# Finer pieces at the two ends of a fused attention and SwiGLU kernel, side work moved and divided, and a list schedule built in 24 passes

## The chip, the cores and the metric

The kernel runs on one core of one Trainium2 chip. The metric is the device time of one execution in microseconds (us). A kernel's time is the median of its runs. The engines are TensorE (matmuls; PE in the profile, its weight loads PEld), VectorE (DVE), ScalarE (ACT), GpSimd (POOL) and SyncE (SP), which issues the transfers.

## The reference, cut to what matters

```python
# x: [1, 2048, 1024] bf16, all weights bf16
xn = layernorm(x)
qkv = xn @ wqkv                                  # 32 heads of 32
phi = lambda t: where(t > 0, t + 1, exp(t)) + 1e-6
kv, z = einsum(phi(k), v), sum(phi(k))           # linear attention: one state per head
s = ((phi(q) @ kv) / (phi(q) @ z + 1e-6)) @ wo
g = silu((silu(xn @ w_gate) * (xn @ w_up)) @ w_down)      # 1024 -> 3584 -> 1024
return x + s * g
```

## The kernel before

The kernel does its large products with seven-product block algorithms (two levels in places), so VectorE and ScalarE have much to do beside TensorE: sums and differences of operand blocks ("combinations"), moves and corrections of the partial results in PSUM. The program is first written down as a list of operations with what each reads and writes. A small list scheduler inside the kernel then builds one fixed instruction stream per engine from its own estimates of times. At run time each engine follows its stream in order.

The rule by which the scheduler picks, for every engine but TensorE:

```python
def schedule(self):
    ...                                  # cut: deadlines o.dl, from TensorE's work and the successors
    while len(order) < total:
        for e in self.ENGS:
            t = free[e]
            ...                          # cut: TensorE, in program order within a window of 6
            rdy = [o for o in a if o.ready <= t]
            o = (min(rdy, key=lambda o: (o.dl - o.boost, o.idx)) if rdy
                 else min(a, key=lambda o: (o.ready, o.dl)))
            ...                          # cut: take the engine that can start first
```

`boost` is zero throughout. The first x tile, its transposes, and the combinations:

```python
def x_load(i):                           # one 256 KB transfer on SyncE's queue
    dma([], [s.r], s.ap(), xf[i * 128:(i + 1) * 128, :], dsem("x%d" % s.k), 256 * KB).urgent = 10.0

# in ln_tile: two statistics over 512 columns, then one normalise over 1024
# in t_tile: tile 0 in two groups of 4 transposes, tiles 1 to 3 in one group of 8;
#            every PSUM copy of the first group goes to ScalarE

def combos(v):                           # four operations over 128 x 2048
    tt(..., v["T3"][0], v["R11"][0], v["R01"][0], ALU.subtract, True)
    tt(..., v["T1"][0], v["R01"][0], v["R00"][0], ALU.subtract, True)
    tt(..., v["T2"][0], v["R11"][0], v["T1"][0], ALU.subtract, True)
    tt(..., v["T4"][0], v["R10"][0], v["T2"][0], ALU.subtract, True)
```

Each `tt` is one elementwise operation on VectorE. Side work is hung on named steps of the block products. `recip` makes the reciprocal of the attention's denominator, `normalise_part` scales q with it (4 ScalarE scalings and 4 VectorE products each time), `combos(QV)` and `x_inner` prepare q for the product with the folded `kv @ wo`:

```python
if (k, n) == ("u", 1):
    at = {"2_1": [partial(recip, p)]}
if n == 2:
    at = {w: [partial(normalise_part, p, "gu".index(k), h)] for h, w in enumerate(("2_1", "7_1"))}
if (k, n) == ("g", 3):
    at = {"2_1": [partial(combos, QV)], "7_1": [partial(x_inner, QV, qin, QIN_AT)]}
```

The program ends by testing every transfer's semaphore on SyncE:

```python
for s in semn.values():
    if id(s) in PL.count:
        prog["sp"].append(("w", s, PL.count[id(s)]))
```

Of the kernel before, what the change touches and what calls it, by code (L numbers as in the profile page):

```python
# [10 lines left out]
ALU = mybir.AluOpType  # L11
# [7 lines left out]
TABLE, DMA_SLACK = 1.28, 2.0  # L19
# [14 lines left out]
class Plan:  # L34
# [71 lines left out]
    def schedule(self):  # L106
# [9 lines left out]
        for o in ops:  # L116
            if o.sem is not None and o.succs:
                k = bisect_right(cum, o.dl - self.lead) - 1
                if k >= 0 and pes[k] not in o.preds:
                    o.preds.add(pes[k])  # L120
                    pes[k].succs.append(o)
        for o in ops:
# [13 lines left out]
        while len(order) < total:  # L136
            best = None
            for e in self.ENGS:
# [17 lines left out]
                else:  # L156
                    rdy = [o for o in a if o.ready <= t]
                    o = min(rdy, key=lambda o: (o.dl - o.boost, o.idx)) if rdy else min(a, key=lambda o: (o.ready, o.dl))
# [29 lines left out]
        return order  # L188
# [55 lines left out]
def build_kernel(nc, A_x, A_wqkv, A_wo, B_w_gate, B_w_up, B_w_down, out, WINDOW=6, NWARM=14, NPE=4, LEAD=12.0):  # L244
# [12 lines left out]
    with ExitStack() as es:  # L257
# [220 lines left out]
        def combos(v):  # L478
            tt([v["R11"][1], v["R01"][1]], [v["T3"][1]], v["T3"][0], v["R11"][0], v["R01"][0], ALU.subtract, True)
            tt([v["R01"][1], v["R00"][1]], [v["T1"][1]], v["T1"][0], v["R01"][0], v["R00"][0], ALU.subtract, True)  # L480
            tt([v["R11"][1], v["T1"][1]], [v["T2"][1]], v["T2"][0], v["R11"][0], v["T1"][0], ALU.subtract, True)
            tt([v["R10"][1], v["T2"][1]], [v["T4"][1]], v["T4"][0], v["R10"][0], v["T2"][0], ALU.subtract, True)
# [179 lines left out]
        def x_load(i):  # L662
            s = x_ring.take()
            xslot[i] = s
            dma([], [s.r], s.ap(), xf[i * 128:(i + 1) * 128, :], dsem("x%d" % s.k), 256 * KB).urgent = 10.0
# [9 lines left out]
        def ln_tile(i):  # L675
# [4 lines left out]
            o0 = dve([s.r], [sA], lambda h: h.bn_stats(stats[:, j, 0, :], xa[:, 0:512]), 512)  # L680
            if i == 1:
                o0.preds.add(first_var[0])
                first_var[0].succs.append(o0)
            dve([s.r], [sB], lambda h: h.bn_stats(stats[:, j, 1, :], xa[:, 512:1024]), 512)
# [8 lines left out]
            if i < 2:  # L693
                dve([s.r, mvr, rsr], [o.r], lambda h: h.tensor_scalar(
                    oa, xa, mv[:, j, 0:1], rstd[:, j, :], ALU.subtract, ALU.mult), 1024, 2.6)
# [10 lines left out]
        def t_tile(i):  # L706
# [10 lines left out]
            for q, halves in enumerate(((0, 4), (4, 4)) if i == 0 else ((0, 8),)):  # L717
                k0, n = halves
                b = tb[(i + q) % 2]
                pb = ps[b][:, 0:n * 64].bitcast(FP16).rearrange("p (k t) -> p k t", t=128)  # L720
                pe_tr([s.r, ident_r], [bank_r[b]],
                      [(pb[:, k, :], xa[:, (k0 + k) * 128:(k0 + k + 1) * 128], ident[:, :]) for k in range(n)])
                xr = xt_r(i, k0, n)
                if q == 0 or i == 0:
# [42 lines left out]
        for q in range(4):  # L767
            pool([], [named("vx1", q), vx_r[q], pool_chain], lambda h, q=q: h.memset(vext[q][:, :, 128:129], 1.0))
# [14 lines left out]
        def p_piece(i, w, j):  # L783
            b = balloc(True)
            for k in range(2):
                ap, r = KVV[w]["R%d%d" % (k, j)]
                pe_mm([xt_r(i, 4 * k, 4), r], [bank_r[b]],
                      [(ps[b][:, :], xt_ap(i, 4 * k + q), ap[:, q, :], k + q == 0, k + q == 4) for q in range(4)])
# [55 lines left out]
        for n, (fn, args) in enumerate(((x_load, (0,)), (x_load, (1,)), (wkv_load, (0, 1, 0)), (wkv_load, (0, 1, 1)),  # L844
# [419 lines left out]
        class Down:  # L1264
# [107 lines left out]
            def do(self, t):  # L1372
# [15 lines left out]
                elif t[-1] == "q":  # L1388
# [3 lines left out]
                    tick()  # L1392
                elif t[0] == "4":
# [3 lines left out]
                else:  # L1397
                    w = int(t[2])
                    self.sets[w].step(int(t[0]))
                    if t[0] == "6":  # L1400
                        self.s3(w)
                    tick()
                for fn in self.at.get(t, ()):
                    fn()

# [7 lines left out]
            def fin(self, w, i, j, g):  # L1413
                p, c = self.p, 2 * self.h + w
                last = (p, c) == (1, 3)
# [29 lines left out]
                def turn():  # L1445
                    if not tbank:
                        tbank.append(balloc_part())
                    b = tbank[0]
                    pb = ps[b][:, 0:256].bitcast(FP16).rearrange("p (m n) -> p m n", n=128)
                    pe_tr([g.r, ident_r], [bank_r[b]], [(pb[:, m, :], g.ap(FP16)[:, m * 128:(m + 1) * 128], ident[:, :])  # L1450
                                                           for m in range(4)])
# [3 lines left out]
                if last and (i, j) == (1, 0):  # L1455
                    defer(2, turn)
# [41 lines left out]

        tbank = []
# [41 lines left out]
        for p in range(2):  # L1541
            for k, n in order:
# [10 lines left out]
                if (k, n) == ("u", 1):  # L1553
                    at = {"2_1": [partial(recip, p)]}
# [85 lines left out]
```

## Time and profile before

| | before |
|---|---|
| time, median of the runs | 726.71 us |
| span of the profiled execution | 725.4 us |
| TensorE busy | 707.0 us, 97% |
| VectorE, ScalarE busy | 633.8 and 402.7 us |
| first useful matmul | 8.1 us |
| TensorE's gaps over 0.3 us between 15 and 705 us | 10, together 8.3 us |
| last matmul to the end | 5.8 us |

The page of the kernel before begins as follows. The first line below has busy time, share of the span and number of instructions of each engine. The lines of digits give the busy share in tenths for 40 slices of the span. The last line is the chain of work that ended last, by engine.

```profile
span 725.4 us, 11190 instructions
PE 707.0 (97%) x4096; PEld 387.4 (53%) x4110; DVE 633.8 (87%) x1501; ACT 402.7 (56%) x773; POOL 14.2 (2%) x35
...
PE   7999999999999999999999999999999999999996
...
DVE  6999968989999998988966999999999989797852
...
PE 87%; DVE 8%; DMA 2%; ACT 1%; issue 1%; SPq 0%; DVEq 0%
```

TensorE is the limit and the only thing to win is its gaps. The page can't size them well: the Trainium skill ("Perfetto Trace Analysis", Per-engine timelines, Tensor Engine Instruction) says that a matmul's end in the profile is estimated and not observed. The start is observed, so the gaps here are distances between matmul starts, less one beat: 216 ns for 512 columns, 109 ns for 256, the medians of this trace. Gaps of exactly one more beat at 512 columns, one every 10 us, are missing records and stay out by the limit of 0.3 us: this trace has 14 of them and 4096 matmul records for 4110 weight loads, 14 too few.

The waits of TensorE between 15 and 705 us in the kernel before (who waited for whom, us in total, times, longest):

```profile
PE ps L233 <- DVE ps L376: 3.6, 6, 1.0
PE ps L233 <- ACT ps L365: 1.8, 2, 0.9
PE ps L233 <- ACT TM L365: 1.0, 1, 1.0
PE ps L233 <- DVE W L376: 0.3, 1, 0.3
```

All are waits for VectorE or ScalarE, not for transfers. Where those engines stand full is shown by the stretches of the kernel before (busy us of each engine in 20 us, then the granted clock, the DMA share and GB/s):

```profile
220.00:240.00 20.00, 18.54 (x102) 9.44 (x100) 19.93 (x47) 19.26 (x40) 0.00 (x0) 1.00 0.48 135
400.00:420.00 20.00, 19.05 (x97) 9.24 (x96) 19.97 (x46) 4.51 (x10) 0.00 (x0) 1.00 0.95 250
```

The columns after the first are PE, PEld, DVE, ACT, POOL. At 220 to 240 us both VectorE and ScalarE are full while q is scaled. The timeline there, kernel before (start, duration, engine, line, what; in brackets the idle time before it and its releaser):

```profile
232.29 1.35 ACT L365 ACTIVATE H<-H,zc 128x512 bf16<-128x512 bf16 x2
...
233.24 1.03 PE L233 MATMUL ps<-X,W 128*128 128x512 f16 x4
233.52 1.10 ACT L365 ACTIVATE TM<-ps 128x512 f16<-128x512 f32 x2
...
234.40 1.22 DVE L376 TENSOR_TENSOR H<-H 128x2048 f16<-128x2048 f16 x1
234.47 0.64 ACT L365 ACTIVATE ps<-ps 128x512 f32<-128x512 f32 x1
...
235.16 1.90 PE L233 MATMUL ps<-X,W 128*128 128x512 f16 x8 [0.90 <-ACT ps L365]
...
235.74 1.22 DVE L376 TENSOR_TENSOR H<-H 128x2048 f16<-128x2048 f16 x1
...
236.87 0.69 DVE L376 TENSOR_TENSOR ps<-ps,TM 128x512 f32<-128x512 f32 x1
...
237.62 1.04 PE L233 MATMUL ps<-X,W 128*128 128x512 f16 x4 [0.56 <-DVE ps L376]
```

Read it as a queue. ScalarE finishes scalings of q (`H<-H,zc`) and two evictions before it comes to the PSUM copy at 234.47 that TensorE waits for, and TensorE loses 0.90 us. Then VectorE runs a combination of 1.22 us at 235.74, and the addition that TensorE waits for starts only when it is over: another 0.56 us. The combination is only half of that wait: the addition's last input, from ScalarE, was there at 236.60 us, so without the combination it would have started some 0.3 us earlier. The Trainium skill ("TensorE: Matmul & The Clock Gate", the table at its head and "Engine queue depths") says that ScalarE's and VectorE's queues are strictly first in, first out; these lines agree, for nothing overtakes the 1.22 us operation.

At the start, kernel before:

```profile
7.36 0.55 POOL L689 TENSOR_TENSOR rstd<-veps,neg_half 128x1 f32<-128x1 f32 x1 [0.97 <-DVE veps L686]
...
8.25 1.23 DVE L376 TENSOR_TENSOR H<-H 128x2048 f16<-128x2048 bf16 x1 [0.97 <-DMA H<-in_A_wqkv_dram]
9.39 0.54 DVE L694 TENSOR_SCALAR W<-W,mv,rstd 128x1024 f16<-128x1024 bf16 x1
...
12.14 0.61 PE L240 MATMUL ps<-ident,W 128*128 128x128 f16 x8
12.34 0.60 ACT L365 ACTIVATE TM<-ps 128x512 f16<-128x512 f32 x1 [1.69 <-PE ps L233]
...
12.83 1.02 ACT L365 ACTIVATE X<-ps 128x1024 f16<-128x1024 f16 x1
...
13.91 5.35 PE L233 MATMUL ps<-H,X 128*128 128x512 bf16 x23 [1.16 <-ACT X L365]
```

TensorE waits 1.16 us for ScalarE's copy of the whole second tile. And at the end, kernel before:

```profile
718.31 0.60 ACT L365 ACTIVATE TM<-ps 128x512 f16<-128x512 f32 x1 [2.42 <-PE ps L233]
718.93 0.43 DVE L376 TENSOR_TENSOR TM<-TM 128x512 f16<-128x512 f16 x1 [2.26 <-ACT TM L365]
...
719.42 0.40 PE L240 MATMUL ps<-ident,TM 128*128 128x128 f16 x4 [1.15 <-DVE TM L376]
719.85 0.42 DVE L376 TENSOR_TENSOR TM<-ps,TM 128x512 bf16<-128x512 f16 x1 [0.49 <-PE ps L240]
```

Behind the last addition (it ends at 720.27) SyncE issues two stores of 256 KB and then runs 47 semaphore waits one after another, from 721.28 to 724.96 us. The views above leave such instructions out; their records in the trace stand about 60 ns apart even where nothing is waited for.

### The profile page before, as it was taken

To read this page: it belongs to the slowest core of one execution; us is meant where nothing else is said; L and a number is where in the kernel's file an instruction comes from. 1 tells how busy PE (TensorE), PEld (TensorE's weight loads), DVE (VectorE), ACT (ScalarE), POOL (GpSimd) and SP (SyncE) were. 2 spreads that over 40 slices of the span, in tenths; PEclk is the share of its full clock that TensorE was granted. 3 is DMA by queue.
4 is the path that set the end of the run, shared out by engine and by line. 5 is a ranking of instruction groups with operands and counts; after the bars stand their busy time and mean duration, and the time that the engine had idled before them with its cause. 6 is when DMAs were issued, how large, how long until landed. Compare 5 with 4: busy or idle time off the path is not lost.

```text
span 725.4 us, 11190 instructions
## 1 busy us (share of the span) xinstructions
PE 707.0 (97%) x4096; PEld 387.4 (53%) x4110; DVE 633.8 (87%) x1501; ACT 402.7 (56%) x773; POOL 14.2 (2%) x35
## 2 busy tenths in 40 slices
PE   7999999999999999999999999999999999999996
PEld 3544445555555555556555454555555555565642
DVE  6999968989999998988966999999999989797852
ACT  3777554887659666654212156766786656531211
POOL 3101000000000000000000000000000000000000
PEclk9999999999999999999999999999999999999998
DMA  9345235145456343326595954231915241747563
GB/s 306 100 88 106 41 116 174 59 135 200 147 159 166 100 139 123 105 67 177 141 187 161 270 149 140 59 117 61 234 59 175 87 145 61 196 114 180 129 150 94
DMA packets 139127, 98.25 MB, mean 135 GB/s; under 512 B 33344, under 2 KB 136000, under 8 KB 139072
## 3 DMA queue, kind: packets, MB, share of 16 engines
q1 hardware_dynamic: 139072, 97.54, 47.9%
q8 instruction: 32, 0.52, 0.3%
q14 instruction: 23, 0.19, 0.1%
HBM read 77.59 MB, written 12.71 MB: 124 GB/s over the span
## 4 chain that ended last, share of the span: by engine, by line
PE 87%; DVE 8%; DMA 2%; ACT 1%; issue 1%; SPq 0%; DVEq 0%
PE ps L233 87%; DVE W L376 2%; DVE H L376 2%; DVE X L376 1%; DMA P<-x_scratch 1%; DMA H<-in_A_wqkv_dram 1%; DVE ps L376 1%; DVE TM L376 1%; SPq L379 0%; DVE P L376 0%; ACT TM L365 0%; ACT H L365 0%; PE ps L240 0%; ACT L365 0%; ACT ps L365 0%
## 5 line engine op out<-in xcount | busy, mean ns | idle before, releaser
L233 PE MATMUL ps<-X,W 128*128 128x512 f16 (+1 forms) x1344 | 289.9, 354 | 3.2 <-DVE ps L376 2.3
L365 ACT ACTIVATE TM<-ps 128x512 f16<-128x512 f32 (+2 forms) x353 | 186.1, 549 | 105.2 <-PE ps L233 103.1
L233 PE MATMUL ps<-H,W 128*128 128x512 f16 (+2 forms) x1090 | 218.4, 351 | 0.7 <-DVE ps L376 0.4
L376 DVE TENSOR_TENSOR W<-W 128x1024 f16<-128x1024 bf16 (+5 forms) x416 | 184.9, 479 | 5.5 <-PE ps L233 4.9
L233 PEld LDWEIGHTS ps<-X,W 128*128 128x128 f16 (+1 forms) x1344 | 130.4, 98 | 108.6 <-DVE ps L376 4.6
L233 PEld LDWEIGHTS ps<-H,W 128*128 128x128 f16 (+1 forms) x1096 | 106.6, 98 | 95.6 <-DVE ps L376 1.4
L365 ACT ACTIVATE ps<-ps 128x512 f32<-128x512 f32 (+1 forms) x172 | 84.7, 492 | 104.8 <-PE ps L233 101.3
L376 DVE TENSOR_TENSOR ps<-ps,TM 128x256 f32<-128x256 f32 (+1 forms) x250 | 130.7, 525 | 13.8 <-PE ps L233 12.5
L233 PE MATMUL ps<-P,W 128*128 128x256 f16 (+1 forms) x516 | 99.8, 319 | 1.2 <-ACT ps L365 0.9
L365 ACT ACTIVATE H<-ps 128x512 f16<-128x512 f32 (+1 forms) x126 | 75.0, 604 | 45.6 <-PE ps L233 45.5
L376 DVE TENSOR_TENSOR H<-H 128x1024 f16<-128x1024 f16 (+6 forms) x110 | 68.9, 640 | 1.1 <-DMA H<-in_A_wqkv_dram 1.0
L365 ACT ACTIVATE TM<-TM 128x512 f16<-128x512 f32 (+1 forms) x61 | 38.0, 629 | 52.6 <-DVE TM L376 52.6
L233 PEld LDWEIGHTS ps<-P,W 128*128 128x128 f16 (+1 forms) x516 | 50.0, 98 | 31.3 <-ACT ps L365 1.6
L233 PE MATMUL ps<-W 128*128 128x256 f16 (+1 forms) x330 | 62.1, 282 | 1.1 <-DVE ps L376 1.0
L376 DVE TENSOR_TENSOR H<-H,TM 128x512 f16<-128x512 f16 x112 | 45.1, 416 | 15.1 <-ACT H L365 14.9
L376 DVE TENSOR_TENSOR TM<-ps,TM 128x512 f32<-128x512 f32 (+1 forms) x60 | 40.7, 678 | 15.6 <-PE ps L233 15.1
L233 PEld LDWEIGHTS ps<-W 128*128 128x128 f16 (+1 forms) x330 | 31.5, 98 | 33.8 <-DVE ps L376 1.9
L233 PE MATMUL ps<-H,X 128*128 128x512 bf16 (+1 forms) x147 | 35.2, 379 | 2.2 <-ACT X L365 1.6
L233 PE MATMUL ps<-H,P 128*128 128x512 bf16 (+1 forms) x108 | 26.4, 379 | 0.1
L376 DVE TENSOR_TENSOR H<-ps,TM 128x512 f16<-128x512 f32 (+1 forms) x35 | 23.8, 680 | 2.2 <-PE ps L233 2.0
L233 PEld LDWEIGHTS ps<-H,X 128*128 128x128 f16 (+1 forms) x150 | 14.2, 98 | 18.5 <-ACT X L365 2.0
L376 DVE TENSOR_TENSOR TM<-TM,W 128x512 f16<-128x512 f16 (+1 forms) x39 | 14.1, 362 | 11.5 <-ACT TM L365 11.4
(95 smaller groups left out, 426.6 us busy)
## 6 DMA issues: line engine op xcount, KB each, us to landing
W<-in_B_w_gate_dram SPq DMA_DIRECT2D x14, 1024.0 KB, 5.3
W<-in_B_w_up_dram SPq DMA_DIRECT2D x13, 1024.0 KB, 5.6
W<-in_B_w_down_dram SPq DMA_DIRECT2D x14, 896.0 KB, 6.3
W<-in_A_x_dram SPq DMA_DIRECT2D x16, 256.0 KB, 3.0
H<-in_A_wqkv_dram SPq DMA_DIRECT2D x8, 512.0 KB, 8.0
H<-r_scratch SPq DMA_DIRECT2D x32, 128.0 KB, 3.8
W<-m_scratch SPq DMA_DIRECT2D x4, 1024.0 KB, 6.0
s_scratch<-TM SPq DMA_DIRECT2D x32, 128.0 KB, 2.6
```

Source lines behind the costliest of these rows:

```text
L233: last = h.matmul(o, l, r, start=st, stop=sp, skip_group_check=True)
L365: q = PL.op("act", reads, writes, lambda h: h.activation(o, i, func, **kw), nel(o) / (1000.0 if "bias" in kw or not isinstance(kw.get("sca ...
L376: return dve(reads, writes, lambda h: h.tensor_tensor(o, a, b, op), nel(o), 1.92 if fast else 0.96)
```

## The change

The intent is to close TensorE's gaps: begin sooner, end in smaller pieces, and give VectorE and ScalarE an order that keeps TensorE fed. It has five parts: start, end, places (where side work is hung), halves (the divided combinations) and search.

Search: the schedule is built 24 times; after each pass, operations that held TensorE up get a `boost` ("lift"), and the pass with the earliest modelled end is kept. An engine may also stay idle for a much more urgent operation that is ready before the chosen one would end ("hold").

```diff
+        best = None
+        for n in range(PASSES):                       # 24
+            end = self.place()
+            if best is None or end < best[0] - 0.01:
+                best = (end, self.order, {o: (o.start, o.done) for o in ops})
+            if n + 1 < PASSES:
+                self.lift()
 ... cut: lift(), which walks back up to 12 steps from every modelled TensorE gap over 0.15 us
-                    o = min(rdy, key=lambda o: (o.dl - o.boost, o.idx)) if rdy else min(a, ...)
+                    while rdy:
+                        o = min(rdy, key=lambda o: (o.dl - o.boost, o.idx))
+                        q = [q for q in soon if q.ready + HOLD < t + o.busy and q.dl - q.boost + YIELD < o.dl - o.boost] if e != "sp" else ()
+                        if not q:
+                            break
+                        rdy.remove(o)
```

Start:

```diff
+            for h, e in enumerate(("sp", "act")):     # x tile 0: two halves on two queues
+                u = s.sub(h * KB, KB)
 ... cut
+            n = (2, 4, 8, 8)[i]                       # transposes per group, by tile
+            for q, k0 in enumerate(range(0, KT, n)):
 ... cut: normalise in two halves; copies shared between ScalarE and VectorE; tile 1's two
 ... statistics both behind tile 0's; first weight block ahead of x tile 1; first product by quarters
```

Halves, and places:

```diff
-            tt(..., v["T3"][0], v["R11"][0], v["R01"][0], ALU.subtract, True)     # and three more
+            for o, a, b in (("T3", "R11", "R01"), ("T1", "R01", "R00"), ("T2", "R11", "T1"), ("T4", "R10", "T2")):
+                for h in range(2):
 ... cut
-                    at = {"2_1": [partial(recip, p)]}
-                if n == 2:
-                    at = {w: [partial(normalise_part, p, "gu".index(k), h)] for h, w in enumerate(("2_1", "7_1"))}
+                    at = {"j1d": [partial(recip, p)]}
+                if (k, n) == ("g", 2):
+                    at = {"j1a": [partial(normalise_part, p, 0, 0)], "2_1": [partial(normalise_part, p, 0, 1)]}
+                if (k, n) == ("u", 2):
+                    at = {"j1a": [partial(normalise_part, p, 1, 0)], "2_1": [partial(normalise_part, p, 1, 1)], "4_1": [partial(combos, QV)]}
                 if (k, n) == ("g", 3):
-                    at = {"2_1": [partial(combos, QV)], "7_1": [partial(x_inner, QV, qin, QIN_AT)]}
+                    at = {"2_1": [partial(x_inner, QV, qin, QIN_AT)]}
```

End: the last down block is done in two halves of 256 columns, each with its own activation, product, transposes and a 128 KB store with a new semaphore (`oz0`, `oz1`).

```diff
+                for h, b in enumerate((self.sets[1].b, self.b2)):
+                    for n in range(0, NPAIR, 2):
+                        pe_mm([wr, tr], [bank_r[b]], [(ps[b][:, 0:256], wv[:, n + k, :],
+                                                       tv[:, k, 256 * h:256 * h + 256], False, n + k == NPAIR - 1)
+                                                      for k in range(2)])
+                        if turns and n == 2:
+                            self.turn0()
+                        if turns and n == 8:
+                            turn(turns.pop())
 ... cut: activation, product, and the turn (transposes, addition, store) of the half
```

More of the change, by code (lines that the diff above doesn't have):

```diff
@@ L16 @@
 GRAN = 256
-TABLE, DMA_SLACK = 1.28, 2.0
+PASSES, LIFT = 24, 2.0
+TABLE, DMA_SLACK, HOLD, YIELD = 1.28, 2.0, 0.1, 10
 class Op:
@@ L121, in schedule, with lift, place @@
                     pes[k].succs.append(o)
+        best = None
[5 more added lines that the diff above has]
+                self.lift()
+        self.order = best[1]
+        for o, (a, b) in best[2].items():
+            o.start, o.done = a, b
+        return self.order
+    def lift(self):
+        prev, last = {}, {}
+        for o in self.order:
+            prev[o] = last.get(o.eng)
+            last[o.eng] = o
+        for o in self.order:
+            p = prev[o]
+            if o.eng != "pe" or p is None or o.start - p.start - p.busy < 0.15:
+                continue
+            c = o
+            for _ in range(12):
+                late = max(c.preds, key=lambda p: p.done, default=None)
+                if late is None:
+                    break
+                if c.eng not in ("pe", "sp") and c.start - max(c.ready, late.done) > 0.02:
+                    c.boost += LIFT
+                c = late
+    def place(self):
+        ops = self.ops
         for o in ops:
@@ L157, in schedule @@
                     rdy = [o for o in a if o.ready <= t]
-                    o = min(rdy, key=lambda o: (o.dl - o.boost, o.idx)) if rdy else min(a, key=lambda o: (o.ready, o.dl))
+                    soon = [o for o in a if o.ready > t]
+                    while rdy:
+                        o = min(rdy, key=lambda o: (o.dl - o.boost, o.idx))
+                        q = [q for q in soon if q.ready + HOLD < t + o.busy and q.dl - q.boost + YIELD < o.dl - o.boost] if e != "sp" else ()
+                        if not q:
+                            break
+                        rdy.remove(o)
+                    if not rdy:
+                        o = min(soon or a, key=lambda o: (o.ready, o.dl))
                 s = max(t, o.ready)
@@ L187, in schedule @@
         self.order = order
-        return order
+        return max(o.done for o in ops)
     def emit(self, esem):
@@ L478, in combos @@
         def combos(v):
-            tt([v["R11"][1], v["R01"][1]], [v["T3"][1]], v["T3"][0], v["R11"][0], v["R01"][0], ALU.subtract, True)
-            tt([v["R01"][1], v["R00"][1]], [v["T1"][1]], v["T1"][0], v["R01"][0], v["R00"][0], ALU.subtract, True)
-            tt([v["R11"][1], v["T1"][1]], [v["T2"][1]], v["T2"][0], v["R11"][0], v["T1"][0], ALU.subtract, True)
-            tt([v["R10"][1], v["T2"][1]], [v["T4"][1]], v["T4"][0], v["R10"][0], v["T2"][0], ALU.subtract, True)
+            for o, a, b in (("T3", "R11", "R01"), ("T1", "R01", "R00"), ("T2", "R11", "T1"), ("T4", "R10", "T2")):
+                for h in range(2):
+                    w = {}
+                    for nm in (o, a, b):
+                        ap, r = v[nm]
+                        n = len(r.keys) // 2
+                        w[nm] = ap[:, 2 * h:2 * h + 2, :], Region(r.keys[n * h:n * h + n])
+                    tt([w[a][1], w[b][1]], [w[o][1]], w[o][0], w[a][0], w[b][0], ALU.subtract, True)
         wz = TM.at(0, 1 * KB, FP16)
@@ L664, in x_load @@
             xslot[i] = s
-            dma([], [s.r], s.ap(), xf[i * 128:(i + 1) * 128, :], dsem("x%d" % s.k), 256 * KB).urgent = 10.0
+            if i:
+                dma([], [s.r], s.ap(), xf[i * 128:(i + 1) * 128, :], dsem("x%d" % s.k), 256 * KB).urgent = 10.0
+                return
+            for h, e in enumerate(("sp", "act")):
+                u = s.sub(h * KB, KB)
+                o, q = u.ap(), xf[0:128, h * 512:h * 512 + 512]
+                PL.op(e, [], [u.r], lambda h, o=o, q=q: h.dma_start(o, q), 0.47, sem=dsem("x%d" % (4 * h)),
+                      nbytes=128 * KB)
         def wkv_load(w, j, k):
@@ L679, in ln_tile @@
             sA, sB, mvr, ver, rsr, nmr = (named(n, j) for n in ("sA", "sB", "mv", "ve", "rs", "nm"))
-            o0 = dve([s.r], [sA], lambda h: h.bn_stats(stats[:, j, 0, :], xa[:, 0:512]), 512)
+            oA = dve([s.sub(0, KB).r], [sA], lambda h: h.bn_stats(stats[:, j, 0, :], xa[:, 0:512]), 512)
+            oB = dve([s.sub(KB, KB).r], [sB], lambda h: h.bn_stats(stats[:, j, 1, :], xa[:, 512:1024]), 512)
             if i == 1:
-                o0.preds.add(first_var[0])
-                first_var[0].succs.append(o0)
-            dve([s.r], [sB], lambda h: h.bn_stats(stats[:, j, 1, :], xa[:, 512:1024]), 512)
+                for o in (oA, oB):
+                    o.preds.add(first_var[0])
+                    first_var[0].succs.append(o)
             dve([sA, sB], [mvr], lambda h: h.bn_aggr(mv[:, j, :], stats[:, j, :, :]), 60)
@@ L693, in ln_tile @@
             if i < 2:
-                dve([s.r, mvr, rsr], [o.r], lambda h: h.tensor_scalar(
-                    oa, xa, mv[:, j, 0:1], rstd[:, j, :], ALU.subtract, ALU.mult), 1024, 2.6)
+                n = 512
+                for c in range(0, 1024, n):
+                    dve([s.r, mvr, rsr], [o.sub(2 * c, 2 * n).r], lambda h, c=c: h.tensor_scalar(
+                        oa[:, c:c + n], xa[:, c:c + n], mv[:, j, 0:1], rstd[:, j, :], ALU.subtract, ALU.mult), n, 2.6)
             else:
@@ L716, in t_tile @@
                 tb.extend((balloc_part(), balloc_part()))
-            for q, halves in enumerate(((0, 4), (4, 4)) if i == 0 else ((0, 8),)):
-                k0, n = halves
-                b = tb[(i + q) % 2]
+            n = (2, 4, 8, 8)[i]
+            for q, k0 in enumerate(range(0, KT, n)):
+                b = (tb + kvb)[q] if i == 0 else tb[(i + q) % 2]
                 pb = ps[b][:, 0:n * 64].bitcast(FP16).rearrange("p (k t) -> p k t", t=128)
-                pe_tr([s.r, ident_r], [bank_r[b]],
+                pe_tr([s.sub(k0 * 256, n * 256).r, ident_r], [bank_r[b]],
                       [(pb[:, k, :], xa[:, (k0 + k) * 128:(k0 + k + 1) * 128], ident[:, :]) for k in range(n)])
                 xr = xt_r(i, k0, n)
-                if q == 0 or i == 0:
+                if q % 2 == 0 or i == 0:
                     act([bank_r[b]], [xr], dst[:, k0:k0 + n], pb, ACT.Identity)
@@ L767, in build_kernel @@
         for q in range(4):
-            pool([], [named("vx1", q), vx_r[q], pool_chain], lambda h, q=q: h.memset(vext[q][:, :, 128:129], 1.0))
+            pool([], [named("vx1", q), vx_r[q], pool_chain], lambda h, q=q: h.memset(vext[q][:, :, 128:129], 1.0), 0.13)
         def k_evac(i, j, ap, r, kind):
@@ L784, in p_piece @@
             b = balloc(True)
-            for k in range(2):
-                ap, r = KVV[w]["R%d%d" % (k, j)]
-                pe_mm([xt_r(i, 4 * k, 4), r], [bank_r[b]],
-                      [(ps[b][:, :], xt_ap(i, 4 * k + q), ap[:, q, :], k + q == 0, k + q == 4) for q in range(4)])
+            n = 2 if (i, w, j) == (0, 0, 1) else 4
+            for k0 in range(0, KT, n):
+                ap, r = KVV[w]["R%d%d" % (k0 // 4, j)]
+                pe_mm([xt_r(i, k0, n), r], [bank_r[b]],
+                      [(ps[b][:, :], xt_ap(i, k), ap[:, k % 4, :], k == 0, k == KT - 1) for k in range(k0, k0 + n)])
             if w == 0:
@@ L842, in kv_set @@
             return st
-        for n, (fn, args) in enumerate(((x_load, (0,)), (x_load, (1,)), (wkv_load, (0, 1, 0)), (wkv_load, (0, 1, 1)),
+        for n, (fn, args) in enumerate(((x_load, (0,)), (wkv_load, (0, 1, 0)), (x_load, (1,)), (wkv_load, (0, 1, 1)),
                                         (wkv_load, (0, 0, 0)), (wkv_load, (0, 0, 1)), (x_load, (2,)),
@@ L1392, in do @@
                     tick()
+                elif t == "4_1" and (self.p, self.h) == (1, 1):
+                    self.finish()
                 elif t[0] == "4":
@@ L1401, in do @@
                         self.s3(w)
+                    if t == "7_1" and (self.p, self.h) == (1, 1):
+                        b = self.sets[1].b
+                        self.b2 = balloc()
+                        act([bank_r[b]], [bank_r[self.b2], bank_r[b]], ps[self.b2][:, 0:256], ps[b][:, 256:512], ACT.Identity)
                     tick()
@@ L1404, in do, with finish, turn @@
                     fn()
+            def finish(self):
+                p, c, (i, j) = 1, 3, (1, 0)
+                wv, wr = self.S[1][4]
+                sf = sf_rings[self.link].take()
+                dma([named("s", p, c, i)], [sf.r], sf.ap(FP16), s_scr[p, c, i, :, j * 512:j * 512 + 512],
+                    dsem("sf%s%d" % (sf.a.name, sf.off // KB)), 128 * KB)
+                g = fin_rings[self.link].take()
+                q, seen = self.xo[1, j]
+                xv = q.ap().rearrange("p (m n) -> p m n", n=256)
+                turns = []
+                def turn(h):
+                    gh = g.sub(h * KB // 2, KB // 2)
+                    b = balloc_part()
+                    pb = ps[b][:, 0:128].bitcast(FP16).rearrange("p (m n) -> p m n", n=128)
+                    pe_tr([gh.r, ident_r], [bank_r[b]], [(pb[:, m, :], gh.ap(FP16)[:, m * 128:(m + 1) * 128],
+                                                          ident[:, :]) for m in range(2)])
+                    v = xv[:, 2 * h:2 * h + 2, :]
+                    vr = q.sub(h * KB, KB).r
+                    tt([bank_r[b], vr], [vr], v[:, :, 128:256], pb, v[:, :, 128:256], ALU.add)
+                    row = p * 1024 + h * 256
+                    dma([vr], [], of[row:row + 256, c * 256:(c + 1) * 256].rearrange("(m p) n -> p m n", p=128), v,
+                        dsem("oz%d" % h), 128 * KB)
+                for h, b in enumerate((self.sets[1].b, self.b2)):
+                    for n in range(0, NPAIR, 2):
+                        tv, tr = self.t4[n // 2]
+                        pe_mm([wr, tr], [bank_r[b]], [(ps[b][:, 0:256], wv[:, n + k, :],
[5 more added lines that the diff above has]
+                            turn(turns.pop())
+                    gh, sh = g.sub(h * KB // 2, KB // 2), sf.sub(h * KB // 2, KB // 2)
+                    act([bank_r[b]], [gh.r], gh.ap(FP16), ps[b][:, 0:256], ACT.Silu)
+                    tt([gh.r, sh.r], [gh.r], gh.ap(FP16), gh.ap(FP16), sh.ap(FP16), ALU.mult, True)
+                    turns.append(h)
+                turn(1)
             def keep(self, w):
@@ L1414, in fin @@
                 p, c = self.p, 2 * self.h + w
-                last = (p, c) == (1, 3)
                 sf = sf_rings[self.link].take()
@@ L1445, in turn @@
                 def turn():
-                    if not tbank:
-                        tbank.append(balloc_part())
-                    b = tbank[0]
+                    b = balloc_part()
                     pb = ps[b][:, 0:256].bitcast(FP16).rearrange("p (m n) -> p m n", n=128)
                     pe_tr([g.r, ident_r], [bank_r[b]], [(pb[:, m, :], g.ap(FP16)[:, m * 128:(m + 1) * 128], ident[:, :])
-                                                           for m in range(4)])
+                                                        for m in range(4)])
                     tt([bank_r[b], q.r], [q.r], xv[:, :, i * 128:i * 128 + 128], pb[:, :, :],
@@ L1454, in turn @@
                     done()
-                if last and (i, j) == (1, 0):
-                    defer(2, turn)
+                if (p, self.h, w, i, j) == (1, 1, 0, 1, 0):
+                    self.turn0 = turn
                 else:
@@ L1497, in down @@
             last_pair[0] = nxt
-        tbank = []
         combos(XV[0])
```

## The prediction

> **What bounds the kernel now.** The profile page has TensorE busy 707.0 of 725.4 us (97%), VectorE 87%, ScalarE 56%; the chain of waits is 87% TensorE. Only gaps in TensorE's stream can be won. By the starts of its 4,096 matmul records (216 ns apart at 512 columns, 109 at 256) they come to about 15 us; lone gaps of one beat, every 10 us, look like missing records and are left out.
>
> - Start, 5 us. Eight warm-up matmuls stand 427 ns apart, then 216: the cold clock of the Trainium skill ("TensorE: Matmul & The Clock Gate", Part 1), and the trace agrees. Then waits for the first normalised tile (transposes at 7.4 us, first useful matmul at 8.1), a weight DMA (0.5, at 11.3), ScalarE's copy of the second transposed tile (1.3, at 13.9).
> - Middle, 8.5 us: at 135 us (1.1; ScalarE's table load), 234-237 and 533-536 (1.8 each; scaling of q, ScalarE and VectorE over 19 busy of 20 us), 415 (1.1; VectorE's order), 438-443 (1.9; table load, VectorE), 655 (0.5).
> - End: 1.3 us before the last transposes. From the last matmul (719.6) to the end, 5.8 us: an addition, two 256 KB stores, and a run of about 48 SyncE waits, 60 ns each, that starts only after the last issue.
>
> **What the change does.**
> 1. Start: x tile 0 comes in halves on two queues, its normalise, transposes and copies go in pieces, and tile 1's statistics no longer delay tile 0's (0.65 us of VectorE): first useful matmul near 6.7 us. Tile 1's transposes move between weight blocks, hiding the weight wait and the copy. TensorE could gain 3 us, but weights stream at 300 GB/s until 20 us, and VectorE is idle only some 2 us between 12 and 83 us. A halved combination costs two operations of 0.68 for one of 1.22 us: +0.14 us, 24 times, 1.1 us of it here. Net 1.8 us.
> 2. Middle: instruction order only. The list schedule is repeated 24 times, lifting what delayed TensorE; the scaling of q moves about half a block pair earlier. The work stays and so do the table loads, so not all closes: 5.5 of 8.5 us.
> 3. End: fourteen 512-column matmuls become 28 of 256 (+0.03 us) with six transposes between (+0.34). The last pass over ScalarE, VectorE, TensorE, VectorE has half the columns: 0.60+0.43+0.41+0.42 becomes about 0.38+0.28+0.29+0.28, -0.6. Only a 128 KB store is left; its semaphore is the newest, so SyncE should test it last, when the store has landed, not in mid-run. Net 1.2 us.
>
> Nearly all of this is on TensorE's chain or behind it: 8.5 us.
>
> **Prediction: 718.5 us; 714.5 to 722.5 holds it 8 times in 10.** Closing every gap would give about 712.5: faster by over 2% has a chance of 0.05, within 2% 0.93, slower 0.02.
>
> **What would show it.** Right: first useful matmul before 7 us, no wait over 0.6 us before 15 us; the waits at 234 and 533 us gone or halved; VectorE busy up about 3 us; TensorE's mid-run gaps down from 8.5 to 3 us; last matmul to end below 5 us. Wrong: an early start, but new waits for VectorE between 20 and 83 us that give it back; or middle gaps moved, not closed.
>
> **What would make it wrong.** The scheduler optimises its own model; where real ScalarE, VectorE or DMA times differ, its picks are luck, and the middle may gain 2 us or 8. Holding an engine for a more urgent operation costs when that comes late. The serial waits may not be sorted as I think.

## The result, and the profile after

The changed kernel took 718.67 us (718.18 to 719.11), the kernel before 726.71 us beside it. The ratio is 0.989, 95% interval 0.9873 to 0.9907. Ratios here are the mean time of one kernel's fast runs over that of the other's in the same rounds, so not quite the ratio of the medians quoted.

The same lines of the page, changed kernel:

```profile
span 716.4 us, 11259 instructions
PE 706.9 (99%) x4114; PEld 389.3 (54%) x4128; DVE 641.5 (90%) x1530; ACT 405.1 (57%) x777; POOL 12.4 (2%) x35
...
PE   8999999999999999999999999999999999999997
...
PE 94%; DVE 3%; DMA 1%; ACT 1%; issue 0%; SPq 0%; DVEq 0%
```

TensorE does the same work in a shorter span. Its waits between 15 and 705 us, changed kernel, have fallen from 6.7 to 1.2 us:

```profile
PE ps L275 <- DVE W L418: 0.6, 1, 0.6
PE ps L275 <- DVE ps L418: 0.4, 1, 0.4
PE ps L275 <- ACT ps L407: 0.2, 1, 0.2
```

The stretch in which q is scaled, changed kernel (columns as above), has ScalarE at 16.15 in place of 19.26 us. The work is moved, not gone: in the 20 us before it, ScalarE has 16.79 in place of 12.81 us.

```profile
220.00:240.00 20.00, 19.82 (x116) 10.91 (x114) 19.90 (x50) 16.15 (x34) 0.00 (x0) 1.00 0.28 94
400.00:420.00 20.00, 19.64 (x105) 10.00 (x104) 19.84 (x51) 7.03 (x13) 0.00 (x0) 1.00 0.74 191
```

Its timeline, changed kernel:

```profile
227.83 1.37 ACT L407 ACTIVATE H<-H,zc 128x512 bf16<-128x512 bf16 x2
...
229.05 0.64 ACT L407 ACTIVATE ps<-ps 128x512 f32<-128x512 f32 x1
...
230.43 3.62 PE L275 MATMUL ps<-X,W 128*128 128x512 f16 x16
...
231.98 0.69 DVE L418 TENSOR_TENSOR ps<-ps,TM 128x512 f32<-128x512 f32 x1
```

Sixteen matmuls run through without a gap: the scalings are over, and VectorE comes to its addition in time. The start, changed kernel:

```profile
6.67 1.21 ACT L407 ACTIVATE X<-ps 128x256 f16<-128x256 f16 x4 [4.18 <-PE ps L282]
...
7.11 1.04 PE L275 MATMUL ps<-H,X 128*128 128x512 bf16 x4
...
11.34 7.08 PE L275 MATMUL ps<-H,X 128*128 128x512 bf16 x31
```

The end, changed kernel:

```profile
710.94 0.38 ACT L407 ACTIVATE TM<-ps 128x256 f16<-128x256 f32 x1 [1.48 <-PE ps L275]
711.36 0.29 DVE L418 TENSOR_TENSOR TM<-TM 128x256 f16<-128x256 f16 x1 [0.23 <-ACT TM L407]
...
711.71 0.28 PE L282 MATMUL ps<-ident,TM 128*128 128x128 f16 x2 [0.80 <-DVE TM L418]
712.03 0.29 DVE L418 TENSOR_TENSOR TM<-ps,TM 128x256 bf16<-128x256 f16 x1 [0.38 <-PE ps L282]
```

By landmarks that both traces have, the 8.9 us between the two profiled spans divide so:

- Start, 1.7 us. The third group of eight transposes begins at 19.10 us before and 18.26 us after, and by then the changed kernel has done 44 useful matmuls in place of 40 (four beats of 216 ns).
- Middle, 6.0 us. The last down block's first matmul comes at 712.06 and at 704.33 us, 7.7 us earlier, of which the start had 1.7.
- End, 1.2 us. From that matmul to the end it is 13.3 us before and 12.1 us after.

Two cautions. The profiled run of the changed kernel was the fastest of its four (718.18 us) and that of before a slow one (727.11 us), so the three terms add up to 0.9 us more than the 8.0 us between the medians. And the start varies from run to run. e4 below runs the same instructions up to the last waits, but its x tile 1 landed at 6.64 in place of 5.76 us, and its third group of transposes begins at 18.77 us, 0.5 us later. TensorE also begins with 14 warm-up matmuls that stand before the first transposes. In the ten traces with the whole finer start, 9 to 13 of them were 427 ns apart and not 216, and the first useful matmul came between 7.1 and 8.1 us; in e9 half of tile 0 was normalised at 6.52 us, but its transposes began at 7.14, one beat after the last warm-up matmul.

### The profile page after: what moved, and what is told of

It is laid out like the page before. It is cut to its first block, busy times and chain, and to the rows that moved or that the text cites. A ratio compares the mean times of both kernels' runs of the same rounds, so it can differ in the third digit from the quotient of the medians.

```text
span 716.4 us, 11259 instructions
## 1 busy us (share of the span) xinstructions
PE 706.9 (99%) x4114; PEld 389.3 (54%) x4128; DVE 641.5 (90%) x1530; ACT 405.1 (57%) x777; POOL 12.4 (2%) x35
## 4 chain that ended last, share of the span: by engine, by line
PE 94%; DVE 3%; DMA 1%; ACT 1%; issue 0%; SPq 0%; DVEq 0%
PE ps L275 94%; DMA H<-in_A_wqkv_dram 1%; DVE W L418 1%; DVE H L418 1%; DVE ps L418 1%; ACT TM L407 0%; PE ps L282 0%; DVE P L418 0%; DVE TM L418 0%; SPq L421 0%; DVE H L811 0%; ACT ps L407 0%; ACT H L407 0%; DVE TM L810 0%; SPq L717 0%
## 5 line engine op out<-in xcount | busy, mean ns | idle before, releaser
L275 PEld LDWEIGHTS ps<-X,W 128*128 128x128 f16 (+1 forms) x1358 | 132.1, 98 | 105.1 <-DVE W L418 1.1
L418 DVE TENSOR_TENSOR ps<-ps,TM 128x256 f32<-128x256 f32 (+1 forms) x250 | 131.3, 528 | 13.3 <-PE ps L275 10.9
L418 DVE TENSOR_TENSOR H<-H 128x1024 f16<-128x1024 f16 (+5 forms) x126 | 70.7, 579 | 0.6 <-ACT H L407 0.2
L418 DVE TENSOR_TENSOR TM<-ps,TM 128x512 f32<-128x512 f32 (+2 forms) x62 | 41.5, 670 | 13.5 <-PE ps L275 12.4
```

The source lines that it names most:

```text
L275: last = h.matmul(o, l, r, start=st, stop=sp, skip_group_check=True)
L418: return dve(reads, writes, lambda h: h.tensor_tensor(o, a, b, op), nel(o), 1.92 if fast else 0.96)
```

## The experiments

Each kernel ran beside the kernel before on one chip, five rounds. Most of them test a part of the change by taking it away or by leaving it alone; e4 and e12 go beyond it. "Loss in the middle" is the sum of TensorE's gaps over 0.3 us between 15 and 705 us in the profiled execution.

| kernel | median us | ratio to before | loss in the middle, us |
|---|---|---|---|
| before | 726.71 | 1 | 8.3 |
| changed | 718.67 | 0.9890 | 1.6 |
| e1 changed, old rule, one pass | 719.67 | 0.9901 | 3.9 |
| e2 before + search | 724.78 | 0.9973 | 5.2 |
| e3 changed, old places | 721.90 | 0.9930 | 5.5 |
| e4 changed, few waits at the end | 716.77 | 0.9862 | 2.1 |
| e5 changed, whole combinations | 718.71 | 0.9889 | 1.6 |
| e6 changed, old start | 719.33 | 0.9900 | 1.8 |
| e7 changed, old end | 719.52 | 0.9900 | 1.6 |
| e8 changed, x tile whole | 719.34 | 0.9907 | 3.8 (profile disturbed) |
| e9 before + start and end | 725.08 | 0.9977 | 9.0 |
| e10 e9 + places | 721.61 | 0.9927 | 4.7 |
| e11 e9 + halves | 722.03 | 0.9938 | 5.8 |
| e12 e4 with 96 passes | 715.71 | 0.9854 | 1.0 |

The 95% intervals of the ratios are 0.0012 to 0.0018 to either side, about 1 us. Each of two kernels has such an interval, so ratios that differ by less than about 0.002 (1.4 us) are not told apart by time alone. e1 to e4 ran on another chip than e5 to e12, each beside the kernel before.

The question that the result leaves open is which part closed the gaps of the middle. Theory A: the 24-pass search. Theory B: the operations moved to earlier places, and divided.

### e1: one pass of the old rule

```diff
-PASSES, LIFT = 24, 2.0
-TABLE, DMA_SLACK, HOLD, YIELD = 1.28, 2.0, 0.1, 10
+PASSES, LIFT = 1, 2.0
+TABLE, DMA_SLACK, HOLD, YIELD = 1.28, 2.0, 0.1, 1e9     # nothing is ever held
```

> The changed kernel with the list schedule of before: one pass, no lifting, no holding of an engine. All pieces and moved operations of the change stay. Theory A (the 24-pass search closes the gaps in the middle, worth 6.4 of the 8 us): 723.5 to 725 us, with gaps of 1 us near 130, 230, 410, 435 and 530 us back in TensorE's stream. Theory B (the moved scaling of q, reciprocal and combinations close them; the search only trims): 718.5 to 720 us, start and tail as in the changed kernel. The new pieces at the start and end stay, so under both the first useful matmul is at 7.1 us.

It took 719.67 us, within Theory B's range and far from A's. Without the search the kernel still keeps 7.2 of its 8.0 us (ratio 0.9901 against 0.9890). The gaps of 1.8 us at 230 and 530 us stay closed. What comes back is the gap of 1.15 us at 134 us (ScalarE's table load), one of 0.54 us at 649 us, and a new one of 0.96 us at 28 us, of which more under e9. The first useful matmul came at 7.6 us and not at 7.1 as expected (11 slow warm-up matmuls in place of 9).

### e2: the search alone

The whole `schedule`, `lift` and `place` of the change put into the kernel before; nothing else.

> The kernel before with nothing but the new list schedule (24 passes, lifting, holding). Theory A: 720 to 721.5 us, the gaps at 134, 234, 415, 438 and 533 us closed. Theory B: 724.5 to 726.5 us; the gaps at 234 and 533 us stay, since the operations are still emitted where they were. The start (first useful matmul 8.1 us) and the tail (5.8 us after the last matmul) stay as before under both.

It took 724.78 us, 2.0 us less than before, as Theory B had it. The gaps near 234 and 533 us stay, as one of 1.5 us each: with the scaling and the combinations emitted where they were, the search did not find an order that keeps them out of TensorE's way. The gap of 1.1 us at 135 us stays as well. The loss in the middle falls by 3.1 us, but the start is 0.7 us later than before, so not all of it is kept. That is this run's transfers and not the search: the first four weight blocks were issued at the same times as in before and each landed 0.7 us later.

### e3: the old places

```diff
-                    at = {"j1d": [partial(recip, p)]}
+                    at = {"2_1": [partial(recip, p)]}
 ... and normalise_part, combos(QV) and x_inner as in the kernel before
```

> The changed kernel, search and all, with only the places of reciprocal, scaling of q, QV combinations and inner sums put back as before. Theory A: 718.5 to 719.5 us. Theory B: 722 to 724 us, with the gaps of 1.8 us near 229 and 525 us back while ScalarE and VectorE are over 19 of 20 us busy there.

721.90 us, just under Theory B's range and far above A's: the places are worth 2.9 us even under the search. The gaps at 234 and 531 us are back, but at half size (0.9 and 1.0 us, two pieces each) and not at the 1.8 us expected. The moves of the reciprocal, the scaling, the combinations and the inner sums were not tried one by one, here or in e10.

### e4: fewer waits at the end

```diff
-        for s in semn.values():
-            if id(s) in PL.count:
+        for n, s in semn.items():
+            if id(s) in PL.count and n[:2] in ("oo", "oz"):
```

Only the stores to the output are waited for at the end. Every other transfer has been waited for by what reads it.

> The changed kernel whose SyncE tests, at the end, only the semaphores of the stores to the output (the other transfers have each been waited for by what reads them). Theory (the 48 serial waits of 60 ns after the last store issue bound the tail, not the store itself): the last store's packets end 1.2 us after its issue and SyncE's run of waits ends 2.0 us after that, so 1.5 to 1.9 us less: about 717.0 us, and last matmul to end near 3.0 us instead of 4.6. Rival (the store's completion or the closing barrier bounds the tail): under 0.4 us less.

716.77 us; the ratio falls by 0.0028, which is 2.0 us, and from the last matmul to the end it is 3.06 in place of 4.68 us. SyncE's own records, read from the two traces (these instructions are in none of the views; start in us):

```
changed kernel                     few waits
712.345 last store issued          713.318 last store issued
712.769 first of 48 waits          713.741 first of 3 waits
715.988 last wait                  715.335 last wait
```

In the changed kernel the run of waits goes on for 3.2 us at 60 ns apiece, with one pause of 0.4 us, whether or not the stores have landed. With three waits the last one is released 2.0 us after the issue, and now the store is the limit. The part of the prediction that put SyncE's run of waits at the end of the chain is shown by this. The stop in mid-run that the prediction speaks of is in the trace before: the 24th of its 47 waits ends 0.55 us after the one before it, at 723.53 us, when the last store has landed (723.52), and 23 waits still follow. In the changed kernel the last store landed at 714.35 us and is tested last, at 715.99, without a stop. So an estimated 0.5 us of the 1.2 us at the end is this stop.

### e5: undivided combinations

> The changed kernel with the combinations of x and q undivided again (one operation of 1.22 us in place of two of 0.68 us). Theory (a long VectorE operation in front of a short urgent one holds up TensorE, and the search cannot cut it): 719.5 to 721 us, with gaps of 0.5 to 1.1 us back near 230, 410 and 525 us. Rival (the places and the search suffice; halves cost 3 us of VectorE for nothing): 718.2 to 718.8 us, VectorE's busy time 3 us lower.

The edit puts back the four `tt` calls of `combos`. 718.71 us, ratio 0.9889 against 0.9890: no difference, as the rival said. But VectorE's busy time fell by 1.1 us only (640.4 against 641.5), not by 3. Two adjacent halves take 1.28 us together against 1.22 us for the whole, since their records of 0.68 us overlap. The Trainium skill ("Perfetto Trace Analysis", Optimizing Scalar/DVE Operations) puts the overhead of one VectorE operation on SBUF at about 60 ns of engine time and says that the profiled latency is about twice that; the 0.06 us measured here agree.

### e6 and e8: the old start, whole and in part

e6 puts back `x_load`, `ln_tile`, `t_tile`, `p_piece` and the order of the first loads; e8 only the loads, the statistics and the normalise:

```diff
-            if i:
-                dma(...).urgent = 10.0
-                return
-            for h, e in enumerate(("sp", "act")):
 ... cut
+            dma([], [s.r], s.ap(), xf[i * 128:(i + 1) * 128, :], dsem("x%d" % s.k), 256 * KB).urgent = 10.0
```

> The changed kernel with the first x tiles loaded, normalised, transposed and copied as before. Theory (the 1.7 us won before 15 us lasts to the end, since nothing behind it was waiting for VectorE): 720.2 to 720.8 us, TensorE's gaps of 0.6 and 1.3 us at 7.4 and 12.5 us back. Rival (VectorE, 97% busy from 20 to 80 us, would have given part of it back): under 1.0 us slower than the changed kernel, and gaps in 20 to 80 us differ between the two.

> The changed kernel with x tile 0 loaded whole on one queue behind which tile 1 follows at once, statistics and normalise as before, but transposes in quarters and copies split over ScalarE and VectorE as in the change. Theory (the wait of 1.3 us for the copy of tile 1 was the larger part): 719.0 to 719.5 us; first useful matmul near 8.0 us, but no gap over 0.6 us after it. Rival (the early x half is the larger part): 720.0 to 720.6 us, as with the whole start put back.

e6: 719.33 us, 0.7 us slower than the changed kernel by the ratios and 0.8 by the profiled spans (717.2 against 716.4). The theory's 1.7 us was too much, and the rival's reason is not what happened: no gap over 0.3 us stands between 15 and 80 us in either. The first useful matmul is late again (8.4 us, with 13 slow warm-up matmuls before it) and the gap of 0.6 us at 7.7 us is back, but the wait for tile 1's copy is 0.4 us and not 1.3. In the kernel before, the normalise of tile 1 stood behind a combination of 1.23 us (the line at 8.25 us shown of before); divided, the combination lets it through. So the parts overlap at the start too. The size of it is rough, as 0.7 us is within the intervals and near the 0.5 us by which the start varies.

e8: 719.34 us, in the range of its theory, but e6 took the same with more put back, so the two halves of the start are not told apart. One of e8's six runs, the profiled one, took 723.2 us (the others 719.0 to 720.4): TensorE stood 2.2 us near 404 us. That run counted as fast, and its profile is not used.

### e7: the old end

> The changed kernel with the last down block whole, as before. Theory: the tail after the last matmul is 5.8 instead of 4.7 us, while TensorE ends 0.3 us earlier for the transposes it does not do: 0.8 to 1.2 us slower, 719.5 to 719.9 us. Rival (the serial waits on SyncE hide all of it): within 0.4 us of the changed kernel.

The edit takes `finish` out and lets the last block run whole. 719.52 us, ratio 0.9900: 0.7 us slower, within the interval of the 0.8 to 1.2 expected. From the last down block's first matmul (704.51 us) to the end (717.84) it is 13.3 us, as in the kernel before, against 12.1 in the changed one. The sum of 1.2 us is confirmed by the traces; the times alone would not have resolved it.

### e9, e10, e11: parts alone, without the search

All three have the old rule in one pass and the finer start and end. e9 has nothing else, e10 has the new places, e11 has the divided combinations.

> The changed kernel with the old list rule in one pass, the old places and undivided combinations: only the finer start and end are left of the change. Theory (start, middle and end are separate sums): 2.4 to 2.9 us faster than before, 724 to 724.5 us, and between 15 and 705 us TensorE loses as much as in the kernel before (5.7 us). Rival (the start's gain needs the divided combinations or the search): under 1.7 us faster.

> As the last, with the new places of reciprocal, scaling of q, QV combinations and inner sums as well; combinations whole, one pass of the old rule. Theory (the places alone close the two gaps of 1.8 us at 234 and 533 us, the search takes the rest): 720.0 to 720.8 us, gaps near 134, 410 and 435 us left. Rival (places need divided combinations or the search): 722 us or more.

> Start and end of the change, divided combinations, old places, one pass of the old rule. Theory (a combination of 1.22 us in front of a short urgent operation is the cause of the gaps at 415 and 234 us in part): 721 to 723 us, the gaps at 234 and 533 us down to about 1 us each. Rival (halves do nothing without the search): 723.5 to 725 us.

e9 took 725.08 us: only 1.7 us faster, below the 2.4 to 2.9 expected and at the edge of the rival's range. The end is in its trace as it should be (4.7 us from the last matmul), and so is the start in that no wait for tile 1's copy is left, though its first useful matmul came at 7.9 us, behind 13 slow warm-up matmuls. But a new gap of 1.03 us stands at 28.4 us that neither the kernel before nor the changed one has. Its timeline:

```profile
24.70 0.63 PE L275 MATMUL ps<-H,TM 128*128 128x129 bf16 x8
...
26.89 1.89 PE L275 MATMUL ps<-H,W 128*128 128x512 f16 x8
...
28.89 0.70 DVE L418 TENSOR_TENSOR ps<-ps,TM 128x512 f32<-128x512 f32 x1 [0.32 <-PE ps L275]
...
29.65 1.04 PE L275 MATMUL ps<-H,W 128*128 128x512 f16 x4 [0.86 <-DVE ps L418]
```

and that of the changed kernel at the same place:

```profile
26.92 1.03 PE L275 MATMUL ps<-H,W 128*128 128x512 f16 x4
...
27.79 0.63 PE L275 MATMUL ps<-H,TM 128*128 128x129 bf16 x8
...
27.99 0.70 DVE L418 TENSOR_TENSOR ps<-ps,TM 128x512 f32<-128x512 f32 x1 [0.25 <-PE ps L275]
28.25 1.02 PE L275 MATMUL ps<-H,X 128*128 128x512 bf16 x4
```

VectorE is not late in e9; it was idle 0.32 us itself. TensorE has nothing to put between a group and the addition that it needs of that group. The one group that would fit, eight small matmuls of the attention state, had been taken at 24.7 us, when TensorE was ahead. The searched order keeps it for this place. The same gap (0.96 to 1.03 us) stands in e1, e10 and e11, all with the early start and one pass, and in the searched e3 as well, so the search does not always find it. So a part of the early start was given back, by order and not by VectorE's load. This is read from the two timelines; moving that group alone was not tried.

e10 took 721.61 us, between its range and the rival's; the places alone, on top of e9, are worth 3.6 us (0.9977 to 0.9927). The gaps at 234 and 533 us are gone, and that at 415 us as well; those at 135 and 437 us are left.

e11 took 722.03 us, in its range: the halves alone are worth 2.8 us on top of e9, the gaps at 234 and 530 us down to 1.0 us each.

With e1, e3, e5 and the changed kernel, which have the same start and end, this shows what each part is worth beside the others:

- Places: 2.7 to 3.6 us, with or without halves or search (e9 to e10, e11 to e1, e3 to changed).
- Search: 2.8 us with places and whole combinations (e10 to e5), but only 0.8 us if the halves are there too (e1 to changed), and 0.6 us with halves and old places (e11 to e3). The last two are within the uncertainty.
- Halves: 2.8 us alone (e9 to e11), 1.9 us with places (e10 to e1), nothing with places and search (e5 to changed).

So with the places moved, search and halves can stand in for each other, and neither stands in for the places.

### e12: one more pass

```diff
-PASSES, LIFT = 24, 2.0
+PASSES, LIFT = 96, 2.0              # and the few waits at the end, as in e4
```

> The changed kernel with 96 passes in place of 24 and the few waits at the end. In the scheduler's own model the best of 96 is pass 25, 0.5 us better than the best of the first 24, and none later is better. If the model's 0.5 us is real: 716.2 to 716.5 us. If differences of that size in the model mean nothing on the chip: 716.3 to 717.8 us, either side of the 716.77 us of the run with few waits alone.

715.71 us, 0.9854 against the 0.9862 of e4. It is the best kernel, with a loss of 1.0 us in the middle. The difference to e4 lies within the intervals, so a gain from the 25th pass is not shown. That both beat the changed kernel, by the end's waits, is.

## Why the prediction was right

The time was within 0.2 us of the predicted 718.5. Point by point:

- **The bound.** Right: only gaps moved. TensorE's busy time is 706.9 against 707.0 us, and its gaps in the middle fell from 8.3 to 1.6 us.
- **Start, 1.8 us predicted, 1.7 measured** by landmarks. No wait over 0.6 us before 15 us, as said; the first useful matmul came at 7.1 us, not before 7. The cause was named in part only: by e6's trace about half of the 1.7 us comes without the finer start, since a divided combination also lets tile 1 through. That the sum fits is partly luck: the prediction had up to 3 us won, less what the stream of weights and VectorE's load would take. The gain by 19 us was only 1.7, and of what the prediction feared, a loss to VectorE's load between 20 and 80 us, the traces show nothing. A give-back of 1.0 us exists (e9), but by the timelines it stems from TensorE's own order.
- **Middle, 5.5 us predicted, 6.0 measured** by landmarks, 6.7 by the gaps over 0.3 us. Both traces lack 14 matmul records, so the 0.7 us between the two is not that; it was not followed further. The waits at 234 and 533 us are gone.
- **End, 1.2 us predicted, 1.2 measured** in the traces: the stop in mid-run is gone, and e4 shows that SyncE's run of waits is what ends last.
- **What the prediction weighed wrongly.** "The list schedule is repeated 24 times, lifting what delayed TensorE" stands first in its account of the middle. The runs show that its worth hangs on the rest: with all else present it adds 0.8 us (e1, itself no larger than the uncertainty; the gaps say 2.2 us), alone 2.0 us (e2), and 2.8 us where the places are moved and the combinations whole (e10 to e5). The places give 3.6 us on e9, and 2.9 us are lost without them (e3). The halves, which the prediction booked as a cost, give 2.8 us on e9, and nothing once places and search are there (e5).
- **The term that was mis-sized.** "A halved combination costs two operations of 0.68 for one of 1.22 us: +0.14 us." Measured: 1.28 against 1.22 us, so 0.06. Adding record lengths counted the overlap of neighbours twice.
- **VectorE busy "up about 3 us".** It rose by 7.7 us, and hardly from the halves: e11 has them at 635.8 us, e9 lacks them at 635.1. All searched kernels stand at 640 to 642 us (e2, 639.7, with no other change). On one chip, e1 and e4 differ by the search and the end's waits, and VectorE's time is 635.4 and 641.5 us. Most of this is how busy time is counted. The lengths of their VectorE records add up to 750.5 and 751.3 us, nearly the same. But records of neighbours overlap, and busy time counts an overlap once. In the searched order VectorE pauses more often and for shorter (212 times in place of 152), so fewer neighbours overlap: 109.8 us in all in place of 115.1, which is 5.3 of the 6.1 us. It cost nothing that the runs show.

Single gains over e9 or before (2.0 + 3.6 + 2.8 us) add up to 8.4 us, and together they bring 6.3 us on e9 (0.9977 to 0.9890). They are cures for the same gaps. That may also be why the sum in the prediction held though its terms were given to the wrong parts: it was built from the gaps that exist, not from the edits.

## What to carry to other kernels

Predict such a change from the list of the bottleneck engine's gaps, and take one part away and put one part in alone before giving any part the credit, for several edits can close the same gap. Where an engine works strictly in order, first move bulky side work to where that engine has slack: in this kernel neither the search nor the division could replace that. Then divide what can stand in front of a short urgent operation, or search for a better order: here either did, and both together hardly more. Look past the last matmul too: serial waits for transfers that others have already waited for cost this kernel 1.6 us after its work was done.

## What the Trainium skill lacked or had wrong

- No page that was read has the cost of a row of semaphore waits at the end of a program. On SyncE they stood 60 ns apart though satisfied: 48 of them took 3.2 us, and leaving out all but those of the output took the stretch from last matmul to end from 4.68 to 3.06 us (e4).
- "Perfetto Trace Analysis", Optimizing Scalar/DVE Operations, advises larger operations on a saturated engine, and breaking them up on one that is not saturated but causes bubbles on others. It doesn't say what to do with an engine that is both full and the cause of bubbles: here VectorE was busy 19.93 of 20 us from 220 to 240 us, dividing a 1.22 us operation cost 0.06 us, and in an order that was not searched it saved 2.8 us (e9 to e11).
- "Perfetto Trace Analysis", Tensor Engine Instruction, says that ends are modelled. It doesn't say that matmul records can be missing: here one beat of 216 ns is lacking about every 10 us in the first 160 us of the trace before, 14 in all, as many as matmul records are fewer than weight loads.
- "TensorE: Matmul & The Clock Gate", Part 1, fits: eight warm-up matmuls 427 ns apart and then 216. In the other traces 9 to 13 of the 14 were slow, which in several of them held up the first useful matmul.
